# A linear-attention and two-mixture kernel: first mixture by 512 tokens in a written order, decays scanned from a chunk's head, memory taken from no shared pool, last four tiles routed inside the first expert

## The chip, the cores and the metric

The kernel runs on one NeuronCore of a Trainium2 chip. The metric is device time in microseconds of one execution; before the change the runs took 990.52, 990.67 and 990.67 us, median 990.67. Five engines work side by side, each through its own queue in order: TensorE (PE, whose weight loads are listed as PEld), VectorE (DVE), ScalarE (ACT), GpSimd (POOL) and SyncE (SP), which issues most DMAs.

## The reference

Three parts follow one another. All inputs are float32.

```
# 1. gated linear attention, batch 4, heads 8, 768 steps, head size 48
state = alpha[t][:, None] * state + outer(k[t], v[t])
y[t] = q[t] @ state                       # gives x: 3072 tokens x 384
# 2. first mixture: three projections to 768, their maximum, one back
h = max(x @ w1, x @ w2, x @ w3)           # 384 -> 768
x = h @ w_out                             # 768 -> 384
# 3. second mixture: 8 experts, the two largest noisy logits of each token
logits = x @ w_gate + log1p(exp(x @ w_noise)) * noise
out[token] += gate * (relu(x @ w1[e]) @ w2[e])     # 384 -> 1024 -> 384
```

## The kernel before

**Attention.** The sequence is cut into 24 units (j), two for each block of 256 tokens. `prep_a(j)` makes the decays with two scans on DVE: one backwards over the decays gives R (from each step to the end of its chunk of 64), a reciprocal of the chunk's product gives the start value of a second, forward one, D. R times the keys (POOL) and D times the queries (DVE, in `prep_x`) make a chunk's work a matmul. `r0`, the product over a chunk, times a decay of the input fills `AE` on POOL, the factors of the chunk-to-chunk scan. `att_t` transposes the keys on PE, `att_s` forms scores of 64 x 64 and masks them on DVE, `att_g` the contribution of each chunk to the state; there DVE scans the state over the chunks (L316), multiplies the result with `AE` (L319), and ACT copies it beside the values. `att_y` gives the output of a unit and splits it into a high and a low part, of reduced float32 (`FR`); for the odd unit six small DMAs (L348) put heads in their place.

**First mixture.** The weights come as float64 words. `wconv(i)`, i from 0 to 11, takes a piece through `dissect`: an absolute value on ACT, a maximum with TINY, a shift and two combinations on DVE (L164 to L167), a cast on ACT to the high part and a subtraction on POOL for the low part. `ffn(u, f)` multiplies block u (256 tokens) with one of six column groups f of three matrices: 3 x 9 matmuls of 256 columns (three contraction parts, each as high x high, high x low, low x high), each matrix into its own PSUM area; ACT copies the first, DVE takes two maxima, ACT casts, POOL subtracts. `proj(u, t)` projects 128 tokens back in 18 matmuls of 400 columns, the last 16 of which are the gate and noise logits.

**Routing.** Tiles of 128 tokens are routed six at a time, in four batches: softplus and noise (`route_a`, `route_b`), ranks within the experts by matmuls with triangular and all-one matrices (`route_c`, `route_r`), and a table of token numbers by one-hot matmuls (`route_h`, `route_m`). Tokens of rank below 384 come from a first table, finished after 18 tiles; the rest after the last batch.

**Second mixture.** Each expert is worked in two halves (n = 2e, 2e + 1) of 384 and 448 slots. `gather` fetches rows by indirect DMA, `turn` transposes them, `esplit` splits the weights, `up` and `down` multiply, and an indirect DMA adds the rows to the output. From n = 1 on a loop mixes the next half's gathers and transposes with this half's matmuls.

**What sets the order.** The program's text gives a sequence of calls for the start (L543 and after), then a loop over u, then a sequence from the last projections to the first expert. A planner of the tile framework puts each engine's instructions into a fixed order when the program is built, by priority (the text's order) and by when its own timing model finds them ready, so the order on an engine is near the text's but not the same. Semaphores do the rest at run time.

**Memory.** Pools are stacks of tiles. `at` holds what attention needs, and the raw pieces and scratch of `dissect` as well; it is closed in the last part of the loop, and `pr`, the experts' pool, takes its place. `pw` holds the first mixture's weights, `p2` the experts' weights after it.

Of the kernel before, what the change touches and what calls it, by code (L numbers as in the profile page):

```python
# [33 lines left out]
LATE = 2304  # L34

TINY = float(np.array([896 << 20], np.uint32).view(np.float32)[0])


@with_exitstack
def gla_moe_kernel(ctx: ExitStack, tc: tile.TileContext, qka, pad, vn, ws, wo, wgn, noise, e1, e2, out):  # L40
# [9 lines left out]
    pw = pw_cm.__enter__()  # L50
    at_cm = tc.tile_pool(name="at", bufs=1, side="right")
# [25 lines left out]
    Z = at.tile([128, 512], F32, name="Z")  # L77
    AE = [at.tile([128, 2, 48, 5], F32, name=f"ae{i}") for i in range(2)]
# [3 lines left out]
    H = ph.tile([128, 2, 6, 2, 256], FR, tag="h", name="H")  # L82
# [13 lines left out]
    def wload(i):  # L96
        if i in (2, 3, 4, 7, 8):
            wraw[i] = RAW[:, (i - 2) % 5]
        else:
            wraw[i] = at.tile([128, 1536], U32, tag="wraw", name="wraw", bufs=2)  # L100
        src = ws[i] if i < 9 else wo[i - 9]
        nc.sync.dma_start(wraw[i], src.bitcast(U32))

    for i in range(2):
        load(i)
        for g in range(2):
            nc.sync.dma_start(QKA[i][64 * g + 48:64 * g + 64], pad)
    for i in range(5):
        wload(i)
    nc.vector.memset(Z, 0.0)  # L110
# [9 lines left out]
    for i in range(2):  # L120
        nc.vector.memset(AE[i], 0.0)
# [35 lines left out]
    def dissect(raw, hi, lo):  # L157
        low, high = raw[:, :, 0], raw[:, :, 1]
        a = at.tile([128, 768], U32, tag="ca", name="ca", bufs=2)
        b = at.tile([128, 768], F32, tag="cb", name="cb", bufs=2)  # L160


        nc.scalar.activation(b, high.bitcast(F32), AF.Abs)
        nc.vector.tensor_scalar(b, b, TINY, None, op0=OP.max)  # L164
        nc.vector.tensor_scalar(a, b.bitcast(U32), 5, 2, op0=OP.logical_shift_left, op1=OP.logical_shift_right)
        nc.vector.scalar_tensor_tensor(a, high, 0xC0000000, a, op0=OP.bitwise_and, op1=OP.bitwise_or)
        nc.vector.scalar_tensor_tensor(a, low, 29, a, op0=OP.logical_shift_right, op1=OP.bitwise_or)  # L167
        f = a.bitcast(F32).rearrange("p (a d) -> p a d", a=2)
# [7 lines left out]
    def wconv(i):  # L176
# [20 lines left out]
    def gates_t(f):  # L197
# [24 lines left out]
    X1, X2, KH, KT, XT, ST, DD = {}, {}, {}, {}, {}, {}, {}  # L222

    parts = {}

    def used(j):
        parts[j] = parts.get(j, 0) + 1
        if parts[j] == 3 and j + 2 < 24:
            load(j + 2)

    def prep_a(j):
# [4 lines left out]

        R = KH[j] = at.tile([128, 512], F32, tag="kh", name="kh", bufs=2)
# [9 lines left out]
        nc.gpsimd.tensor_mul(AE[i][:, :, :, 1:5],  # L247
                             a0.rearrange("p (a b) -> p a b", a=2)[:, :, None, :].to_broadcast([128, 2, 48, 4]),
                             r0[:, :, None, :].to_broadcast([128, 2, 48, 4]))
        used(j)  # L250

    def prep_x(j):
# [18 lines left out]
    def prep_v(j):
# [25 lines left out]
    def att_g(j):  # L297
        i = j % 2

        ps = pa.tile([128, 2, 48, 5], F32, tag="a", name="psG")  # L300
# [9 lines left out]
        if (j // 2) % 3 == 0:  # L310
            nc.vector.memset(ps[:, :, :, 0], 0.0)
        else:
            nc.vector.tensor_copy(ps[:, :, :, 0], ST[j - 2][:, :, :, 4])
        st = at.tile([128, 2, 48, 5], F32, tag=f"S{i}", name="st")
        ST[j] = st
        nc.vector.tensor_tensor_scan(st.rearrange("q p e c -> q (p e c)"), AE[i].rearrange("q p e c -> q (p e c)"),  # L316
                                     ps.rearrange("q p e c -> q (p e c)"), 0.0, op0=OP.mult, op1=OP.add)

        nc.vector.tensor_mul(st[:, :, :, 0:4], st[:, :, :, 0:4], AE[i][:, :, :, 1:5])  # L319
        P = st[:, :, :, 0:4].rearrange("q p e c -> q p c e")  # L320
        nc.scalar.copy(LA[i][64:128, :, :, 0:48], P[64:128])  # L321
        nc.scalar.copy(LB[i][0:64, :, :, 0:48], P[0:64])

    def att_y(j):
        i, u = j % 2, j // 2
        ps = pa.tile([128, 2, 256], F32, tag="a", name="psY")
        for p in range(2):
            for c in range(4):
                s = slice(64 * c, 64 * c + 64)
                sx = slice(256 * p + 64 * c, 256 * p + 64 * c + 64)  # L330
                nc.tensor.matmul(ps[0:64, p, s], LA[i][:, p, c], X1[j][:, sx], start=True, stop=True)  # L331
                nc.tensor.matmul(ps[64:128, p, s], LB[i][:, p, c], X2[j][:, sx], start=True, stop=True)  # L332
        if i == 0:
            XT[u] = pw.tile([128, 3, 2, 256], FR, tag="xt", name="xt", bufs=2)
            x = XT[u]
            nc.scalar.copy(x[:, 0:2, 0, :], ps)
            nc.vector.tensor_sub(x[:, 0:2, 1, :], ps, x[:, 0:2, 0, :].bitcast(F32))
        else:
            x = XT[u]
# [3 lines left out]
            nc.scalar.copy(x[:, 2, 0, :], ps[:, 0])  # L343
            nc.vector.tensor_sub(x[:, 2, 1, :], ps[:, 0], x[:, 2, 0, :].bitcast(F32))

            for o in (0, 64):
                for k in range(3):
                    nc.sync.dma_start(x[o + 48:o + 64, k].bitcast(F32),  # L348
# [6 lines left out]
    def ffn(u, f):  # L355
        x = XT[u]
        p12 = pm.tile([128, 2, 256], F32, tag="p12", name="p12")
        p3 = pm.tile([128, 2, 256], F32, tag="p3", name="p3")
        for w, ps in ((0, p12[:, 0]), (1, p12[:, 1]), (2, p3[:, 0])):
# [5 lines left out]
        m = pw.tile([128, 256], F32, tag="m", name="m", bufs=2)  # L365
        nc.scalar.copy(m, p12[:, 0])  # L366
        nc.vector.tensor_max(m, p12[:, 1], m)  # L367
        nc.vector.tensor_max(m, p3[:, 0], m)  # L368
        hi = H[:, u % 2, f, 0]
        nc.scalar.copy(hi, m)  # L370
        nc.gpsimd.tensor_sub(H[:, u % 2, f, 1], m, hi.bitcast(F32))  # L371

    def proj(u, t):
        ps = pl.tile([128, 400], F32, tag="l2", name="psl2")
        n = 0
        for f in range(6):
            for a, b in THREE:
                nc.tensor.matmul(ps, H[:, u % 2, f, a, 128 * t:128 * t + 128], WOT[0][:, b, f],  # L378
                                 start=n == 0, stop=n == 17)
                n += 1  # L380
        i = 2 * u + t
# [27 lines left out]
    def route_b(b):  # L409
        t, l = RT[b]  # L410
        nl = NL[b]

        u = small([128, 6, NE], "u")
        d = small([128, 6, NE], "d")
# [5 lines left out]
        nc.vector.tensor_mul(l, l, nz[:, 6 * b:6 * b + 6, :])  # L420
        nc.vector.tensor_add(l, l, nl[:, :, 0:8])
        mx = small([128, 6, NE], "mx")
        ix = small([128, 6, NE], "ix", U32)
        for j in range(6):
            nc.vector.max(mx[:, j], l[:, j])
            nc.vector.max_index(ix[:, j], mx[:, j], l[:, j])
        xf = small([128, 6, 2], "xf")
        nc.vector.tensor_copy(xf, ix[:, :, 0:2])
        oh = small([128, 6, 2, NE], "oh")
        nc.vector.tensor_tensor(oh, iota[:, None, 0:NE].to_broadcast([128, 12, NE]).rearrange("p (j k) e -> p j k e", k=2),  # L430
                                xf[:, :, :, None].to_broadcast([128, 6, 2, NE]), op=OP.is_equal)
# [73 lines left out]
    def route_m(b, q):  # L505
# [7 lines left out]
        if q < 2:  # L513
            return
# [482 lines left out]
```

## Time and profile before

| what | value |
|---|---|
| median of the runs | 990.67 us |
| profiled execution | 989.96 us, its span 988.3 us |
| PE busy | 913.0 us, 92% of the span |
| DVE, ACT, POOL busy | 514.6, 389.5, 329.3 us |
| DMA | 88.22 MB, mean 89 GB/s |
| 72 feed-forward groups (L363) | 1944 matmuls, 254.7 us |
| experts, up (L792) and down (L806) | 1152 and 1344 matmuls, 242.5 and 243.3 us |

Busy times of engines overlap and do not add up to the span. A busy PE is one with a matmul in its pipeline; two matmuls start closer than each lasts, so a row's mean duration is not its cost: the distance of two starts is. Idle time of an engine costs nothing unless the last chain of work waits there.

### The profile page before, as it was taken

To read this page: it belongs to the slowest core of one execution; us is meant where nothing else is said; L and a number is where in the kernel's file an instruction comes from. 1 tells how busy PE (TensorE), PEld (TensorE's weight loads), DVE (VectorE), ACT (ScalarE), POOL (GpSimd) and SP (SyncE) were. 2 spreads that over 40 slices of the span, in tenths; PEclk is the share of its full clock that TensorE was granted. 3 is DMA by queue.
4 is the path that set the end of the run, shared out by engine and by line. 5 is a ranking of instruction groups with operands and counts; after the bars stand their busy time and mean duration, and the time that the engine had idled before them with its cause. 6 is when DMAs were issued, how large, how long until landed. Compare 5 with 4: busy or idle time off the path is not lost.

```text
span 988.3 us, 17871 instructions
## 1 busy us (share of the span) xinstructions
PE 913.0 (92%) x7186; PEld 866.7 (88%) x7187; DVE 514.6 (52%) x1040; ACT 389.5 (39%) x801; POOL 329.3 (33%) x362
## 2 busy tenths in 40 slices
PE   2358999999999999999898999999999999999994
PEld 2347999999999999999897999999999999999993
DVE  7999847786668865772573333322333323333110
ACT  3645454455445534632542333332333332333220
POOL 5477524322322332112108333333333233221112
PEclk9979899999999999999999999999999999999998
DMA  9642223134234232104325444334434434422112
GB/s 266 171 137 70 60 55 87 46 106 121 57 82 122 75 81 64 31 13 137 139 87 123 113 105 101 78 79 115 110 98 108 94 60 109 113 57 25 21 25 29
DMA packets 36693, 88.22 MB, mean 89 GB/s; under 512 B 8640, under 2 KB 25024, under 8 KB 36608
## 3 DMA queue, kind: packets, MB, share of 16 engines
q1 hardware_dynamic: 25600, 66.39, 23.7%
q0 software_dynamic: 11008, 20.67, 12.0%
q8 instruction: 57, 0.93, 0.4%
q14 instruction: 28, 0.23, 0.1%
HBM read 64.52 MB, written 20.16 MB: 86 GB/s over the span
## 4 chain that ended last, share of the span: by engine, by line
PE 74%; issue 4%; DMA 3%; DVE 2%; POOL 0%; ACT 0%; POOLq 0%; ACTq 0%; DVEq 0%
PE psd L806 21%; PE psu L792 21%; PE p L363 18%; PE psl L378 5%; DMA out_dram<-y,idx 2%; PE psx L773 2%; PE psS L290 1%; PE psG L306 1%; PE psY L331 1%; PE psT L282 1%; DMA xt<-sg 1%; PE psY L332 1%; DVE kh L239 0%; DVE x L259 0%; DMA xg<-x2d,idx 0%
## 5 line engine op out<-in xcount | busy, mean ns | idle before, releaser
L363 PE MATMUL p<-xt,W 128*128 128x256 f32 x1944 | 254.7, 289 | 9.9 <-DVE m L367 7.3
L363 PEld LDWEIGHTS p<-xt,W 128*128 128x128 f32 x1944 | 241.9, 195 | 15.0 <-DVE m L367 8.1
L792 PE MATMUL psu<-xe,ew 128*128 128x448 f32 (+1 forms) x1152 | 242.5, 358 | 4.3 <-ACT xe L775 4.3
L806 PE MATMUL psd<-ew,he 128*128 128x384 f32 (+1 forms) x1344 | 243.3, 335 | 0.0
L806 PEld LDWEIGHTS psd<-ew,he 128*128 128x128 f32 (+1 forms) x1344 | 227.0, 180 | 8.1 <-ACT y L809 0.2
L792 PEld LDWEIGHTS psu<-xe,ew 128*128 128x128 f32 x1152 | 208.2, 190 | 13.9 <-ACT xe L775 4.7
L796 DVE SCALAR_TENSOR_TENSOR he<-psu,he 128x448 fp32r<-128x448 f32 (+1 forms) x128 | 75.5, 590 | 265.0 <-ACT he L795 265.0
L811 POOL DMA_INDIRECT out_dram<-y,idx x56 | 88.1, 1573 | 187.8 <-ACT y L809 176.2
L371 POOL TENSOR_TENSOR H<-m,H 128x256 fp32r<-128x256 f32 x72 | 60.1, 835 | 191.2 <-ACT H L370 187.1
L809 ACT ACTIVATE y<-psd,GS 128x384 f32<-128x384 f32 (+1 forms) x56 | 32.4, 580 | 206.1 <-PE psd L806 195.2
L795 ACT ACTIVATE he<-psu 128x448 fp32r<-128x448 f32 (+1 forms) x128 | 66.3, 518 | 112.3 <-PE psu L792 112.3
L378 PE MATMUL psl<-WO,H 128*128 128x400 f32 x432 | 84.7, 349 | 0.0
L378 PEld LDWEIGHTS psl<-WO,H 128*128 128x128 f32 x432 | 76.7, 188 | 2.1 <-issue 1.3
L739 DVE TENSOR_TENSOR ew<-raw,ew 128x768 fp32r<-128x768 f32 x64 | 57.2, 954 | 33.6 <-ACT ew L738 32.9
L758 POOL DMA_INDIRECT xg<-x2d,idx x56 | 58.5, 1045 | 43.2 <-PE psx L773 21.2
L367 DVE TENSOR_TENSOR m<-p,m 128x256 f32<-128x256 f32 x72 | 29.9, 417 | 60.4 <-ACT m L366 59.9
L370 ACT CAST H<-m 128x256 fp32r<-128x256 f32 x72 | 29.2, 406 | 68.0 <-DVE m L368 66.2
L777 POOL COPY GS<-xg 128x1 f32<-128x1 f32 (+1 forms) x56 | 10.8, 272 | 124.2 <-DMA xg<-x2d,idx 124.2
L366 ACT COPY m<-p 128x256 f32<-128x256 f32 x72 | 26.4, 369 | 61.6 <-PE p L363 58.4
L738 ACT CAST ew<-raw 128x768 fp32r<-128x768 f32 x64 | 48.6, 831 | 3.2 <-DMA raw<-in_e_dram 3.2
L331 PE MATMUL psY<-x,la 128*64 128x64 f32 x384 | 31.5, 237 | 15.6 <-ACT la L321 14.9
L331 PEld LDWEIGHTS psY<-x,la 128*64 128x64 f32 x384 | 27.1, 148 | 19.7 <-ACT la L321 15.7
(151 smaller groups left out, 1080.0 us busy)
## 6 DMA issues: line engine op xcount, KB each, us to landing
raw<-in_e_dram SPq DMA_DIRECT2D x32, 768.0 KB, 5.6
qka<-in_qka_dram SPq DMA_DIRECT2D x48, 289.7 KB, 4.7
out_dram<-z SPq DMA_DIRECT2D x5, 960.0 KB, 4.5
vn<-in_vn_dram SPq DMA_DIRECT2D x24, 192.0 KB, 2.6
x2d<-x2t SPq DMA_DIRECT2D x24, 192.0 KB, 1.9
RAW<-in_ws_dram SPq DMA_DIRECT2D x5, 768.0 KB, 10.8
wraw<-in_ws_dram SPq DMA_DIRECT2D x4, 768.0 KB, 8.6
xt<-sg SPq DMA_DIRECT2D x72, 32.0 KB, 3.5
```

The costliest lines, as they stand in the source:

```text
L331: nc.tensor.matmul(ps[0:64, p, s], LA[i][:, p, c], X1[j][:, sx], start=True, stop=True)
L363: nc.tensor.matmul(ps, W[:, f, w, a, k], x[:, k, b], start=n == 0, stop=n == 8)
L371: nc.gpsimd.tensor_sub(H[:, u % 2, f, 1], m, hi.bitcast(F32))
L378: nc.tensor.matmul(ps, H[:, u % 2, f, a, 128 * t:128 * t + 128], WOT[0][:, b, f], start=n == 0, stop=n == 17)
L738: nc.scalar.copy(hi, r)
L739: nc.vector.tensor_sub(EW[e, m][:, 1, s], r, hi.bitcast(F32))
L758: nc.gpsimd.indirect_dma_start(out=XG[n, i][0:w], out_offset=None, in_=x2d if h else x2d[0:128 + LATE], in_offset=bass.IndirectOffsetOnAxi ...
L792: nc.tensor.matmul(ps, w[:, a, f, k], XE[n][:, k, b], start=i == 0, stop=i == 8)
L795: nc.scalar.activation(hi, ps, AF.Relu)
L796: nc.vector.scalar_tensor_tensor(HE[n][:, f, 1], ps, 0.0, hi.bitcast(F32), op0=OP.max, op1=OP.subtract)
L806: nc.tensor.matmul(ps, HE[n][:, f, a, o:o + m], w[:, b, f], start=j == 0, stop=j == 23)
L811: nc.gpsimd.indirect_dma_start(out=out, out_offset=bass.IndirectOffsetOnAxis(ap=IDX[h][0:m, 1, c:c + 1], axis=0), in_=y, in_offset=None, c ...
```

## The change

The start-up: the first two units come from a new input, `qk2`, already padded to 128 partitions, in three DMAs each (decays, keys, queries); the pad's DMAs and the memory clearing of `AE` on DVE go. Later loads hang on `prep_x` (queries, keys, decays) and `prep_v` (values) separately. The decays: the forward scan D now runs first and starts from the chunk's first decay; the reciprocal of its last value starts the backward scan. `AE` (now one tile) holds the chunk products alone, filled by ACT; the state's scan adds, then multiplies, so that the product after it goes. The maximum of `dissect` moves to POOL, and scratch and raw pieces get memory of their own. The feed-forward runs over 512 tokens (d from 0 to 5), in one matmul each, except d = 0 and f = 0, 1 of d = 1, which run as two halves. H lies in eight places. Routing has five batches (6, 6, 6, 2 and 4 tiles). The calls stand as words in three lists: a, x, v, t, s, g, y are the attention's functions, w `wconv`, f `ffn`, p `proj`, i and j the gates, z `zero_rows`, r the next routing step; in the last list L, G, E, T, U, D are `eload`, `gather`, `esplit`, `turn`, `up`, `down` and A, B, C, R, H, M the routing of the last four tiles. The last list is run under a manual schedule for PE, DVE and ACT: their instructions keep the text's order.

```diff
+BATCH = (0, 6, 12, 18, 20, 24)
+HANDOVER = """
+    L0.0.0 L0.0.1 L0.1.0 G0.0 G0.1 G0.2 E0.0.0 E0.0.1 p5.0 E0.0.2 E0.0.3 p5.1 T0.0 T0.1 T0.2 E0.1.0 E0.1.1
+    p5.2 E0.1.2 E0.1.3 p5.3 A4 B4 U0.0 U0.1 U0.2 C4 R4 U0.3 H4.0 U0.4 H4.1 U0.5 M4.0 U0.6 M4.1
+    G1.0 G1.1 G1.2 G1.3 G2.0 G2.1 G2.2 U0.7 D0.0 D0.1 T1.0 T1.1 D0.2 T1.2 T1.3
+"""
+ORDER = """
+    a0 x0 t0 a1 s0 v0 g0 x1 s1 a2 t1 y0 v1 x2 g1 a3 y1 w0 v2 w1 w2 t2 s2 x3 g2 v3 w3 w4 t3 s3 y2 g3 a4
+    x4 v4 y3 f0.0.0 w5 f0.1.0 w6 f0.2.0 w7 f0.3.0 t4 s4 w8 f0.4.0 a5 g4 x5 v5 f0.5.0 w9 t5 s5 f0.0.1 a6
...
+    v14 f2.3 z1 r t14 s14 f2.4 r a15 y13 g14 x15 v15 f2.5 r t15 s15 a16 y14 g15 x16 v16 y15 t16 s16
+    f3.0 z2 a17 g16 x17 v17 f3.1 t17 s17 p2.0 a18 y16 g17 x18 v18 p2.1 t18 s18 p2.2 a19 y17 g18 x19 v19
...
+ORDER2 = """
+    f5.0 f5.1 p4.0 p4.1 r p4.2 r r p4.3 r r f5.2 r r f5.3 r r f5.4 r r f5.5 r r
 def load(j):
-        for g in range(2):
-            nc.sync.dma_start(QKA[i][64 * g:64 * g + 48], qka[j, g])
-        nc.sync.dma_start(VN[i].rearrange("p a b c e -> p (a b c e)"), vn[j])
+            for a, b in ((1024, 1545), (512, 1024), (0, 512)):
+                nc.sync.dma_start(QKA[i][:, a:b], qk2[j, :, a:b])
 def dissect(raw, hi, lo):
-        a = at.tile([128, 768], U32, tag="ca", name="ca", bufs=2)
-        b = at.tile([128, 768], F32, tag="cb", name="cb", bufs=2)
+        b = cv.tile([128, 768], F32, tag="cb", name="cb", bufs=2)
+        a = b.bitcast(U32)
-        nc.vector.tensor_scalar(b, b, TINY, None, op0=OP.max)
+        nc.gpsimd.tensor_scalar(b, b, TINY, None, op0=OP.max)
 def prep_a(j):
-        nc.vector.memset(Z[:, 0:512:64], 1.0)
-        nc.vector.tensor_tensor_scan(R[:, ::-1], al[:, 512:0:-1], Z, 0.0, op0=OP.mult, op1=OP.add)
-        nc.vector.reciprocal(Z[:, 0:512:64], R[:, 0:512:64])
-        nc.vector.tensor_tensor_scan(D, al[:, 0:512], Z, 0.0, op0=OP.mult, op1=OP.add)
-        nc.gpsimd.tensor_copy(r0.rearrange("p a b -> p (a b)"), R[:, 0:512:64])
+        nc.vector.tensor_copy(Z[0][:, 0:512:64], a0)
+        nc.vector.tensor_tensor_scan(D, al[:, 0:512], Z[0], 0.0, op0=OP.mult, op1=OP.add)
+        nc.vector.reciprocal(Z[1][:, 63:512:64], D[:, 63:512:64])
+        nc.vector.tensor_tensor_scan(R[:, ::-1], al[:, 512:0:-1], Z[1][:, ::-1], 0.0, op0=OP.mult, op1=OP.add)
         nc.gpsimd.tensor_mul(R, t[:, 512:1024], R)
-        nc.gpsimd.tensor_mul(AE[i][:, :, :, 1:5],
...
+        nc.vector.tensor_copy(EN[j].rearrange("p a b -> p (a b)"), D[:, 63:512:64])
 def att_g(j):
+        nc.scalar.copy(AE[:, :, :, 1:5], EN[j][:, :, None, :].to_broadcast([128, 2, 48, 4]))
+        nc.vector.memset(ps[:, :, :, 0], 0.0)
+        if not first:
+            before = ST[j - 2][:, :, :, 4]
+            nc.scalar.copy(LA[i][64:128, :, 0, 0:48], before[64:128])
+            nc.scalar.copy(LB[i][0:64, :, 0, 0:48], before[0:64])
+            nc.vector.tensor_add(ps[:, :, :, 1], ps[:, :, :, 1], before)
-        nc.vector.tensor_mul(st[:, :, :, 0:4], st[:, :, :, 0:4], AE[i][:, :, :, 1:5])
-    def ffn(u, f):
+    def ffn(d, f, half=None):
+        s = slice(0, 512) if half is None else slice(256 * half, 256 * half + 256)
+        for w in range(3):
+            ps = pm.tile([128, 512], F32, tag="p", name="p", bufs=4)[:, s]
...
+    run(ORDER)
+    at_cm.__exit__(None, None, None)
+    pr = ctx.enter_context(tc.tile_pool(name="pr", bufs=1, side="right", reuse_waits="tile"))
+    run(ORDER2)
...
+    with tc.manual_schedule(engines={mybir.EngineType.PE, mybir.EngineType.DVE, mybir.EngineType.Activation}):
+        run(HANDOVER)
```

## Rows read from the trace of the kernel before

**Rows 1.** The page: span, and PE's busy time.
```profile
span 988.3 us, 17871 instructions
...
PE 913.0 (92%) x7186; PEld 866.7 (88%) x7187; DVE 514.6 (52%) x1040; ACT 389.5 (39%) x801; POOL 329.3 (33%) x362
```

**Rows 2.** Busy time by stretch: start and end, length, engines' busy us (count), clock, DMA.
```profile
0.00:110.00 110.00, 59.63 (x610) 54.49 (x611) 102.66 (x134) 49.97 (x92) 65.64 (x66) 0.89 0.57 153
...
160.00:460.00 300.00, 296.96 (x3151) 282.25 (x3150) 209.24 (x517) 141.06 (x323) 86.53 (x110) 1.00 0.32 82
...
480.00:530.00 50.00, 42.94 (x244) 39.74 (x242) 31.17 (x109) 22.92 (x44) 9.60 (x10) 0.95 0.44 139
```

**Rows 3.** Timeline of the first 12.5 us, DVE's first scan.
```profile
8.57 1.23 DVE L239 TENSOR_TENSOR_SCAN kh<-qka,Z 128x512 f32<-128x512 f32 x1 [5.22 <-DMA qka<-in_pad_dram]
```

**Rows 4.** DMA view of 0 to 30 us, rate in 40 slices of 0.75 us.
```profile
GB/s 0 0 115 338 181 187 123 199 239 181 190 157 187 129 160 296 156 238 401 451 401 410 418 418 426 418 401 426 410 377 370 198 165 194 125 224 224 157 189 144
```

**Rows 5.** DVE's groups, 0 to 110 us: count, busy us, mean ns, idle before.
```profile
L242 DVE TENSOR_TENSOR_SCAN D<-qka,Z 128x512 f32<-128x512 f32 x7 | 13.3, 1902 | 0.1
...
L164 DVE TENSOR_SCALAR cb<-cb 128x768 f32<-128x768 f32 x11 | 8.0, 723 | 0.0
...
L319 DVE TENSOR_TENSOR st<-st,ae 128x384 f32<-128x384 f32 x5 | 4.5, 892 | 0.0
...
L313 DVE COPY psG<-st 128x96 f32<-128x96 f32 x3 | 1.0, 317 | 0.0
...
L238 DVE MEMSET Z<- 128x8 f32 x8 | 0.5, 65 | 0.0
```

**Rows 6.** POOL's groups, 0 to 110 us.
```profile
L170 POOL TENSOR_TENSOR W<-ca,W 128x768 fp32r<-128x768 f32 x9 | 19.4, 2166 | 16.7 <-ACT W L169 16.7
...
L247 POOL TENSOR_TENSOR ae<-qka,r 128x384 f32<-128x384 f32 x6 | 9.5, 1591 | 0.8 <-DVE st L319 0.5
...
L244 POOL COPY r<-kh 128x8 f32<-128x8 f32 x7 | 5.2, 742 | 17.9 <-DVE kh L239 17.9
...
L123 POOL MEMSET la<- 64x512 f32 x2 | 1.0, 520 | 0.1
```

**Rows 7.** Timeline of DVE and of POOL near 40 us.
```profile
39.79 2.09 DVE L164 TENSOR_SCALAR cb<-cb 128x768 f32<-128x768 f32 x1
...
38.75 2.71 POOL L170 TENSOR_TENSOR W<-ca,W 128x768 fp32r<-128x768 f32 x1
```

**Rows 8.** Chain that ended last: start, length, what, count of instructions.
```profile
460.12 19.45 PE p L363 x162
...
580.33 4.18 PE psd L806 x24
584.51 1.85 PE psu L792 x9
```

**Rows 9.** Timeline of PE at the last of these, with its columns.
```profile
584.35 1.81 PE L792 MATMUL psu<-xe,ew 128*128 128x448 f32 x8
```

**Rows 10.** Timeline of PE in the handover, idle before in brackets.
```profile
479.39 3.43 PE L378 MATMUL psl<-WO,H 128*128 128x400 f32 x18
...
494.21 8.15 PE L792 MATMUL psu<-xe,ew 128*128 128x384 f32 x36 [3.89 <-ACT xe L775]
...
524.26 0.52 PE L773 MATMUL psx<-ident,xg 128*128 128x128 f32 x3 [1.31 <-DMA xg<-x2d,idx]
...
528.05 1.54 PE L792 MATMUL psu<-xe,ew 128*128 128x448 f32 x4 [0.41 <-ACT xe L775]
```

**Rows 11.** Timeline of the last batch's routing: first on ACT, one-hot sums on DVE.
```profile
494.41 0.26 ACT L404 ACTIVATE r_t<-nl 128x48 f32<-128x48 f32 x1
...
504.52 0.20 DVE L433 TENSOR_TENSOR r_ob<-r_oh 128x48 bf16<-128x48 f32 x1
```

**Rows 12.** Chain that ended last, near 350 us.
```profile
347.10 0.38 ACT m L366
...
347.99 5.97 DMA xt<-sg
```

More of the change, by code (lines that the diff above doesn't have):

```diff
@@ L105, in gla_moe_kernel @@
         load(i)
-        for g in range(2):
-            nc.sync.dma_start(QKA[i][64 * g + 48:64 * g + 64], pad)
+        load_v(i)
     for i in range(5):
         wload(i)
-    nc.vector.memset(Z, 0.0)
+    for z in Z:
+        nc.vector.memset(z, 0.0)
     nc.gpsimd.memset(ident, 1.0)
@@ L119, in gla_moe_kernel @@
     nc.vector.memset(VBD, 0.0)
-    for i in range(2):
-        nc.vector.memset(AE[i], 0.0)
+    nc.gpsimd.memset(AE, 0.0)
     for i in range(2):
@@ L333, in att_y, with att_y_lo @@
+        if i == 0 and u % 2 == 0:
+            XT[d] = XW2[d % 2]
+    def att_y_lo(j):
+        i, u = j % 2, j // 2
+        d, s = u // 2, slice(256 * (u % 2), 256 * (u % 2) + 256)
+        ps = YP.pop(j)
         if i == 0:
[L334 to L337, printed above, removed]
+            x = XT[d][:, 0:2, :, s]
+            nc.scalar.copy(x[:, :, 0], ps)
+            nc.vector.tensor_sub(x[:, :, 1], ps, x[:, :, 0].bitcast(F32))
@@ L364, in ffn, with proj @@
                     n += 1
[L365 to L369, printed above, removed]
+            if w == 0:
+                nc.scalar.copy(m, ps)
+            else:
+                nc.vector.tensor_max(m, ps, m)
+        hi, lo = (place(d, f)[:, a, s] for a in range(2))
         nc.scalar.copy(hi, m)
-        nc.gpsimd.tensor_sub(H[:, u % 2, f, 1], m, hi.bitcast(F32))
-    def proj(u, t):
+        nc.gpsimd.tensor_sub(lo, m, hi.bitcast(F32))
+    def proj(d, t):
         ps = pl.tile([128, 400], F32, tag="l2", name="psl2")
@@ L410, in route_b @@
         t, l = RT[b]
[L411 to L414 removed]
+        n = BATCH[b + 1] - BATCH[b]
+        nl = NL[b][:, 0:n]
+        u = row("u", b, NE)
+        d = row("d", b, NE)
         nc.vector.tensor_scalar(u, t, 1.0, None, op0=OP.add)
@@ L465, in route_r @@
         xf, oh, rk, ct = RT[b]
-        rb = small([128, 6, NE], "rb")
+        n = BATCH[b + 1] - BATCH[b]
+        rb = row("u", b, NE)
         if b == 0:
@@ L511, in route_m @@
             A, C = held.pop(0)
-            nc.tensor.matmul(ps[:, 0:n], A, C[:, 0:n], start=q == 0 and i == 0, stop=q == 2 and i == 3)
-        if q < 2:
+            nc.tensor.matmul(ps[:, 0:n], A, C[:, 0:n], start=q == 0 and i == 0, stop=q == last and i == 3)
+        if q < last:
             return
@@ new lines, in gla_moe_kernel, with run @@
+    steps = []
+    CALL = {"a": prep_a, "x": prep_x, "v": prep_v, "t": att_t, "s": att_s, "g": att_g, "y": att_y, "w": wconv,
+            "f": ffn, "p": proj, "i": gates_t, "j": gates_m, "z": zero_rows, "c": late_consts}
+    def run(order):
+        for word in order.split():
+            if word == "r":
+                while steps and next(steps[0], steps) is steps:
+                    steps.pop(0)
+                continue
+            args = [int(n) for n in word[1:].split(".") if n]
+            CALL[word[0]](*args)
+            if word[0] == "p" and 4 * args[0] + args[1] + 1 in BATCH:
+                steps.append(routing(BATCH.index(4 * args[0] + args[1] + 1) - 1))
```

488 lines of the change are left out of this document (157 added, 331 removed).

## The prediction

> **What bounds the kernel now.** I read the page first. Its span is 988.3 us and TensorE (PE) is busy for 913.0 of it [rows 1]. So PE is the bound, and a change can only save time in two ways: fewer or faster matmul columns, or fewer PE holes. The second view, busy time by stretch, says where the holes are [rows 2]. From 160 to 460 us PE is busy for 296.96 of 300 us at a granted clock of 1.00 (2.4 GHz; the 0.89 of the first 110 us mixes that level with 1.2 GHz): nothing there is to be had but speed of the matmuls themselves. In the first 110 us PE is busy for 59.63 and VectorE (DVE) for 102.66: the start-up belongs to DVE, which never rests. Between 480 and 530 us, where the mixture hands over to the experts, PE is busy for 42.94 of 50. After that come the experts, whose steady loop the diff leaves alone (only the name of four PSUM banks changes), and I give them nothing.
>
> **Step 1, the first transfer.** The first scan on DVE starts at 8.57 us and has waited 5.22 us for the pad's DMA, the last of five [rows 3]. The change sends the decays (521 of 1545 columns, all 128 partitions, 267 KB) ahead as one DMA; the first scan now needs only these. By the DMA view 86 KB had moved by 2.25 us and 340 KB by 3.0 (115 and 338 GB/s in slices of 0.75 us) [rows 4]. With about 1 us until the queue's receipt wakes DVE I take 4.3 us for the scan's start, which is 4.3 us earlier; the ends are 0 (the pieces share the rings as before) and 5.2 (the whole wait goes). The k and q pieces, 262 KB each at some 190 GB/s, land 1.4 us after one another, within the 2.7 us that the two scans and the reciprocal take.
>
> **Step 2, DVE's work in the start-up.** Of the rows of DVE up to 110 us [rows 5] two disappear: the maximum with TINY (L164, 11 in this stretch, 8.0 us), which moves to GpSimd (POOL), and the product of the state with the decays (L319, 5, 4.5 us), which the scan with the operations in the order add, multiply now yields by itself. New on DVE are a copy of 8 columns per unit in place of a memset of 65 ns, another of 8 columns, and, where a state is carried in, a memset beside an addition of 96 columns that takes the place of a 317 ns copy. A new 8-column operation lies between 65 ns (that memset) and 317 ns (the copy of 96); I take 100 ns, near the memset of its own size, 7 x 100 = 0.7 us, and 0.6 for the carried states: 1.3 us. Net 12.5 - 1.3 = 11.2 us off an engine that has no hole, while PE waits for it; as long as PE starves, that is time. Two guards. First, POOL: its rows lose the copy of r (L244, 7, 5.2 us) and the product for ae (L247, 6, 9.5 us), 14.7 us together, and gain 11 maxima of 768 columns [rows 6]. One of these is bounded by 0.78 us (a memset of 512 columns takes 520 ns, by columns) and 2.17 us (the subtraction of two inputs, L170); 1.3 us, because it reads one input and not two, gives 14 us. So POOL's load stays as it is. That matters since POOL slows DVE: the same maximum took 2.09 us on DVE while POOL's L170 ran for 2.71 us [rows 7], against a mean of 723 ns [rows 5], and the D scan's mean of 1902 ns is of the same origin. With equal POOL load I leave DVE's other rows as they are. Second, ScalarE (ACT) takes over the filling of ae (a copy of 384 columns per unit) and small copies for the carried state; it is busy 49.97 of 110 us [rows 2], so I cost them at nothing; if DVE's order put them ahead of the state's copies, each would delay one unit by under a microsecond. Ends for this step: 0 (POOL holds DVE up for what it takes over) and 20 (POOL's removal also frees DVE's other rows).
>
> **Step 3, 512 tokens in one matmul.** Feed-forward d = 0 runs in halves, and so do f = 0 and 1 of d = 1; the other 28 (4 of d = 1, 24 of d = 2 to 5) are full width: 28 x 27 = 756 matmuls of 512 columns in place of 1512 of 256. The chain of work has 162 of 256 columns in 19.45 us, 120.1 ns each, 24 of 384 in 4.18 us, 174.2 ns, and nine of 448 in 1.85 us, 205.6 ns [rows 8, 9]. No row has 512. From 256 to 384 a column costs 0.42 ns, which gives 174.2 + 54 = 228 ns; in proportion to 448 it is 235 ns, in proportion to 256 it is 240. I take 231, between the two nearest rows: each pair saves 2 x 120.1 - 231 = 9.2 ns, 756 x 9.2 = 7.0 us, with ends 0 and 9.2. All of it is on PE, in the stretch where PE has no hole, so it counts in full. Evictions on ACT and DVE are fewer and longer; DVE is at 209 of 300 us there [rows 2], which covers them. The projections, the attention's matmuls and the gates keep their counts.
> The Trainium skill (TensorE: Matmul & The Clock Gate, Back-to-back issue gap) gives the isolated warm gap as N / 2.4 + 2.5 ns. By it a pair costs 2 x 109.2 and one of 512 costs 215.8, an estimate from that page, so a pair saves 2.6 ns and the step 2.0 us. The trace does not agree at 256 columns, 120.1 ns [rows 8].
>
> **Step 4, the handover.** From the first projection after the last feed-forward to the first matmul of the second half-expert PE takes 528.05 - 479.39 = 48.7 us, with holes of 3.89 (for xe, whose cast stands on ACT behind weights that had not landed), 1.31 us (for the first of the gathers, which start after the routing's end), three of under 0.7 for the others, and 0.41 [rows 10]: some 7 us. The written order sets the transposes before the last two projections, and the gathers under two down-projections, 4.2 us each [rows 8]; that ends both kinds. It also fixes PE, DVE and ACT in one order, with new waits: the rank matmuls of the last 4 tiles stand behind three up-groups (3 x 9 x 174 ns = 4.7 us), while their input needs two table loads and some 16 DVE operations. In the trace of before that took from 494.41 to 504.72 us [rows 11], 10.3 us for 6 tiles; for 4 I take 4/6 of it, 6.9, a hole of 2.2 us, and 2.5 more for the two places where the table's matmuls wait for DVE's one-hot rows. Behind the waiting rank matmul on PE stand all up-groups, and behind DVE's wait the evictions that free the four banks. 7 - 4.7 = 2 us gained, rounded. Ends: 7 (no new hole) and -10 (the chain is not covered at all).
>
> **Sum.** 988.3 - 4.3 - 11.2 - 7.0 - 2.0 = 963.8 us of span. The profiled execution took 989.96 us, 1.7 beside its span, and the median of the runs is 990.67, 0.7 above it: 963.8 + 1.7 + 0.7 = 966 us.
>
> **Rivals.** (a) POOL eats the start-up. If a maximum on POOL costs what L170 does, 11 x 2.17 = 23.9 us replace 14.7, and DVE is held up by them; for it speaks the 2.09 us of [rows 7]. Step 2 is then worth nothing: 977 us. Against it: one input only, and r and ae are gone from the same unit's path.
> (b) More than forecast. If a one-input POOL instruction leaves DVE alone, the loss of r and ae (14.7 of POOL's 65.64 us [rows 2, 6]) frees DVE: the D scans have a mean of 1.90 us where the first scan, with POOL idle, took 1.23 [rows 3, 5], 7 x 0.67 = 4.7 us. With all holes of step 4 gone another 5, and wide matmuls at 228 ns another 2: 954 us.
> (c) The spacing goes with the columns alone, so that one of 512 takes what two of 256 do, 240 ns: step 3 is worth nothing, 973 us. The fixed part in the rows of 256 and 384 (0.469 and 0.454 ns a column) speaks against it. The Trainium skill's gap rule, weighed in step 3, is close to it: 971 us, an estimate.
> (d) Slower: each block of 512 tokens waits for its last x. A full-width group can't start before four units are through, and the last of these ends in six small DMAs; once in the trace the chain went from 347.10 to 353.96 us through an eviction and such a DMA [rows 12], 6.9 us. If PE has nothing to put under it at the five block starts (d = 1 to 5), that is 34 us against 24.5 gained: 1000 us. It decides from the fourth uncovered block on (27 us). For it: in the written order the last unit of d = 3 stands right ahead of that block's first group. Against it: four projections of the block before (3.43 us each [rows 10]) wait to be run there, and in the other blocks at least one full group lies between.
> That the written order is not followed is no rival by itself: outside the handover the planner places instructions by its own timing, and there PE is full anyway.
>
> **How the numbers follow.** Forecast (956 to 975 us) 0.40, (a) 0.22, (b) 0.20, (c) 0.08, (d) 0.10. Range 946 to 986: it holds (a), (b) and (c) and leaves out (d), with some room for ends beyond the cases. A measurement of this kernel can tell 0.2%, 2 us. Faster 0.87 (all but (d), less what of (a) ends at no gain), same 0.03, slower 0.10.
>
> **What would show it.** Step 1: the first scan at 4 to 5 us. Step 2: no product behind the state's scan on DVE, DVE's rows up to 95 us some 11 us lighter, and PE full from about 95 us instead of 110; wrong, if POOL's maximum shows 2 us or DVE's D scan grows beyond 1.9 us. Step 3: 27 matmuls of a full-width group in 6.2 us. Step 4: the time from the first projection after the last feed-forward to the second half-expert, less one projection, 47 us. The forecast is wrong if PE shows holes over 3 us at a block's start, waiting for x, or over 5 us in the handover, waiting for DVE.

## The result, and the profile after

The changed kernel takes 982.4 us (median of four runs, 981.70 to 983.48) against 990.67: ratio 0.9905, interval 0.9886 to 0.9925. The forecast was 966, a gain of 24.7 us; the gain is 8.3. The sign is right, the size a third. The profiled execution took 981.72 us, with a span of 980.0.

Busy time by stretch comes first, with the columns of [rows 2]: the kernel after, then the row of before for 110 to 160 us, which the forecast had not looked at.

```profile
0.00:110.00 110.00, 67.06 (x702) 59.73 (x703) 99.19 (x137) 59.97 (x117) 79.86 (x64) 0.84 0.54 153
110.00:160.00 50.00, 44.06 (x518) 40.86 (x518) 39.35 (x64) 30.58 (x68) 24.11 (x21) 0.97 0.32 73
160.00:460.00 300.00, 297.24 (x2413) 250.60 (x2412) 186.71 (x476) 139.96 (x300) 54.13 (x46) 1.00 0.30 77
480.00:530.00 50.00, 44.67 (x251) 42.63 (x250) 28.15 (x94) 19.72 (x39) 18.23 (x26) 0.97 0.51 140
```

```profile
110.00:160.00 50.00, 48.89 (x530) 47.06 (x531) 29.72 (x52) 25.76 (x58) 19.98 (x19) 1.00 0.20 53
```

POOL went from 65.64 to 79.86 us in the first 110, DVE only from 102.66 to 99.19. And in 110 to 160 us, where PE had been full before, it now has 5.9 us of holes instead of 1.1. The granted clocks of the first 110 us (0.89 before, 0.84 after) can't be compared: from 0 to 40 us the kernel before reads 1.00, yet a pair of its score matmuls (64 x 64) takes 107 ns at 14.4 us and 58 ns at 316 us.

How far one kernel is ahead of the one before is read by a **lead**: each matmul is given its usual distance to the next at full clock (120 ns for 256 columns, 240 for 512, counted as the two that it replaces, 182 for 400, 109 for 128, some 30 for one of 64 columns, and so on), these are added up from the start, and the lead at a time is how much later the kernel before had as much behind it. After is ahead by 8.1 us at 20 us, 6.5 at 100, and **4.9 us behind at 160**; then it comes to +5.5 at 460 and +8.9 at 540, and little moves after that (8.5 at 950). The lead at 160 us moves by about 1 us with the prices of the small matmuls, since the new order has run more of them by then; from 460 us on it does not. The start-up, forecast to end 15.5 us ahead, ended behind; the stretch of the wide matmuls (160 to 460 us) gave 10.4 and that of the handover (460 to 540 us) 3.4.

DVE's start, by the timeline (compare [rows 3]); POOL's groups and DVE's groups up to 110 us (compare [rows 5, 6]); and what PE waited for up to 160 us (us in total, times, longest):

```profile
3.81 0.17 DVE L275 COPY Z<-qka 128x8 f32<-128x8 f32 x1 [0.94 <-DMA qka<-in_qk_dram]
4.01 1.22 DVE L277 TENSOR_TENSOR_SCAN D<-qka,Z 128x512 f32<-128x512 f32 x1
```

```profile
L205 POOL TENSOR_SCALAR cb<-cb 128x768 f32<-128x768 f32 x11 | 32.4, 2949 | 7.2 <-ACT cb L204 7.2
L211 POOL TENSOR_TENSOR W<-cb,W 128x768 fp32r<-128x768 f32 x9 | 18.2, 2025 | 3.9 <-ACT W L210 3.9
```

```profile
L206 DVE TENSOR_SCALAR cb<-cb 128x768 uint32<-128x768 uint32 x10 | 12.5, 1252 | 4.6 <-POOL cb L205 4.5
L277 DVE TENSOR_TENSOR_SCAN D<-qka,Z 128x512 f32<-128x512 f32 x8 | 12.4, 1546 | 0.1
...
L275 DVE COPY Z<-qka 128x8 f32<-128x8 f32 x9 | 4.1, 459 | 2.5 <-DMA qka<-in_qka_dram 1.6 <-DMA qka<-in_qk_dram 0.9
...
L283 DVE COPY en<-D 128x8 f32<-128x8 f32 x8 | 2.8, 355 | 0.0
```

```profile
PE psT L323 <- POOL kh L281: 22.5, 3, 8.6
PE psY L383 <- ACT la L366: 12.0, 5, 4.7
```

The maximum (L205) takes 2.95 us on POOL, more than the subtraction of two inputs beside it. DVE's shift (L206) waits for it, and POOL's product for the keys (L281) is queued behind it: PE's transposes wait 22.5 us for that product. The first of these three waits, 8.6 us, is the start itself: POOL's first maximum comes at 14.7 us. So the maximum can have a part in 13.9 us of it, not in all.

### The profile page after: what moved, and what is told of

Same layout as the page of the kernel before. It is cut to its first block, busy times and chain, and to the rows that moved or that the text cites. A ratio compares the mean times of both kernels' runs of the same rounds, so it can differ in the third digit from the quotient of the medians.

```text
span 980.0 us, 16245 instructions
## 1 busy us (share of the span) xinstructions
PE 908.2 (93%) x6431; PEld 825.8 (84%) x6432; DVE 499.2 (51%) x1014; ACT 400.6 (41%) x806; POOL 317.6 (32%) x299
## 4 chain that ended last, share of the span: by engine, by line
PE 76%; DVE 7%; DMA 6%; issue 2%; ACT 1%; POOL 1%; SPq 0%; POOLq 0%; DVEq 0%; ACTq 0%
PE psd L742 22%; PE psu L728 21%; PE p L432 18%; PE psl L447 6%; DMA qka<-in_qka_dram 3%; DMA out_dram<-y,idx 2%; PE psY L383 2%; PE psx L709 2%; PE psS L331 1%; DVE x L291 1%; PE psG L349 1%; PE psT L323 1%; DVE st L363 1%; DMA raw<-in_e_dram 1%; DVE x L334 1%
## 5 line engine op out<-in xcount | busy, mean ns | idle before, releaser
L432 PE MATMUL p<-xt,W 128*128 128x512 f32 (+1 forms) x1188 | 247.2, 362 | 6.4 <-DVE m L437 3.2
L432 PEld LDWEIGHTS p<-xt,W 128*128 128x128 f32 x1188 | 197.6, 194 | 39.1 <-DVE m L437 3.5
L440 POOL TENSOR_TENSOR H<-m,H 128x512 fp32r<-128x512 f32 (+1 forms) x34 | 43.0, 1264 | 117.1 <-ACT H L439 117.0
L437 DVE TENSOR_TENSOR m<-p,m 128x512 f32<-128x512 f32 (+1 forms) x88 | 51.7, 588 | 48.5 <-PE p L432 40.5
L447 PE MATMUL psl<-WO,H 128*128 128x400 f32 x336 | 68.3, 348 | 0.0
L281 POOL TENSOR_TENSOR kh<-qka,kh 128x512 f32<-128x512 f32 x24 | 33.6, 1399 | 106.5 <-issue 31.8
L447 PEld LDWEIGHTS psl<-WO,H 128*128 128x128 f32 x336 | 60.1, 188 | 1.6 <-issue 0.5
L383 PE MATMUL psY<-x,la 128*64 128x64 f32 x384 | 33.6, 239 | 12.9 <-ACT la L366 12.0
L383 PEld LDWEIGHTS psY<-x,la 128*64 128x64 f32 x384 | 27.9, 148 | 18.1 <-ACT la L366 13.2
L439 ACT CAST H<-m 128x512 fp32r<-128x512 f32 (+1 forms) x34 | 18.5, 545 | 55.2 <-DVE m L437 55.1
```

The source lines that it names most:

```text
L383: nc.tensor.matmul(ps[0:64, p, sc], LA[i][:, p, c], X1[j][:, sx], start=True, stop=True)
L432: nc.tensor.matmul(ps, W[:, f, w, a, k], x[:, k, b], start=n == 0, stop=n == 8)
L437: nc.vector.tensor_max(m, ps, m)
L447: nc.tensor.matmul(ps, place(d, f)[:, a, 128 * t:128 * t + 128], WOT[0][:, b, f], start=n == 0, stop=n == 17)
```

## The experiments

Times against the kernel before, run beside them on the same chip; lead at 160, 460 and 540 us, and PE's idle time up to 160 us (160 less its busy time), from one profiled execution each. The runs of one kernel spread by up to 10 us (lazy 989.78 to 1000.07, max_dve 975.75 to 983.02), and the profiled execution is not always near the median: it took 983.05 us in planned, 983.36 in warm, 991.33 in old_decays and 975.75 in max_dve. Two kernels count as different here where their intervals lie apart.

| kernel | us | ratio, interval | leads | idle |
|---|---|---|---|---|
| before | 990.5 to 991.7 | 1 | 0, 0, 0 | 51.5 |
| after | 982.40 | 0.9905, 0.9886 to 0.9925 | -4.9, 5.5, 8.9 | 48.9 |
| max_dve | 977.45 | 0.9881, 0.9860 to 0.9902 | 1.5, 11.5, 14.5 | 41.3 |
| no_max | 977.48 | 0.9850, 0.9829 to 0.9870 | 2.8, 13.6, 12.2 | 41.3 |
| before_pool | 998.18 | 1.0079, 1.0064 to 1.0093 | -4.5, -4.5, -8.1 | 54.5 |
| halves | 995.73 | 1.0046, 1.0031 to 1.0060 | -4.4, -3.9, -5.5 | 48.9 |
| lazy | 992.42 | 1.0020, 1.0003 to 1.0036 | -1.2, -6.1, -2.9 | 42.7 |
| copies_act | 977.07 | 0.9860, 0.9839 to 0.9882 | 4.3, 9.6, 12.8 | 42.4 |
| old_decays | 987.80 | 0.9982, 0.9962 to 1.0002 | -7.9, -3.5, -0.6 | 47.8 |
| planned | 979.31 | 0.9883, 0.9866 to 0.9899 | -9.2, 0.9, 6.8 | 49.5 |
| first_load | 983.48 | 0.9917, 0.9903 to 0.9931 | 7.5, 7.7, 7.8 | 44.1 |
| warm | 977.92 | 0.9854, 0.9839 to 0.9870 | see there | 37.6 |
| best | 973.76 | 0.9819, 0.9805 to 0.9833 | 0.1, 10.1, 14.6 | 43.0 |
| load_decays | 988.22 | 0.9971, 0.9949 to 0.9994 | 9.0, -0.3, 0.2 | 44.2 |
| old_order | 975.18 | 0.9841, 0.9824 to 0.9858 | -2.0, 8.0, 13.2 | 39.5 |

**max_dve, no_max, before_pool: who takes the maximum.** The edit of max_dve; no_max drops the line, and before_pool is the reverse in the kernel before.

```diff
-        nc.gpsimd.tensor_scalar(b, b, TINY, None, op0=OP.max)
+        nc.vector.tensor_scalar(b, b, TINY, None, op0=OP.max)
```

> The changed kernel with one edit: the maximum of the splitting helper goes back from POOL to DVE. Theory A (POOL's maximum, 2.95 us each, holds POOL's k products and with them TensorE's transposes in the first 110 us): PE's wait for POOL's kh (22.5 us in three waits) shrinks to under 8 us, the first mixture matmul comes 6 to 12 us earlier than 54.9, and the time falls to 970 to 976 us. Rival B (the written order and the other edits of the start-up set its length, whoever takes the maximum): first mixture matmul within 3 us of 54.9, time 980 to 984 us. Rival C (DVE is the tighter engine there, so the move to POOL helped after all): 985 to 995 us.

> The changed kernel with the maximum of the splitting helper left out altogether (a weight under the smallest normal number is then not lifted to it, a part of the computation that is left out). Neither POOL nor DVE has it. Theory A: the whole cost of the maximum goes, 966 to 974 us, a few us under the kernel that has it on DVE. Rival B (order and other edits): 979 to 983 us.

> The kernel before with one edit, the converse: its maximum goes from DVE to POOL. Theory A: POOL's maximum takes 2 to 6 us there as well, POOL goes from 66 to about 90 us busy in the first 110 us, the k products come late: 998 to 1008 us against 990.7. Rival B: no change or, since DVE was the tighter engine there, faster: 982 to 991 us.

The direction of theory A holds both ways: on POOL the maximum costs the changed kernel 5.0 us by the medians and the kernel before 7.6 (998.18 against 990.54, although DVE lost a row there). The intervals of after and max_dve overlap; the clear pair is planned and best, below, which differ in this line alone: 979.31 against 973.76, 5.5 us, with intervals apart. It is not all of it. 977.45 lies between the ranges of A and B, and so does the first mixture matmul, which comes at 50.0 us, 4.9 earlier. PE still waits 18.8 us for POOL's kh in max_dve, 8.5 of them at the start, and leaving the maximum out gives no more than taking it back to DVE (the intervals overlap). So the maximum is the smaller part of the 20.4 us (15.5 forecast, -4.9 found) that the start-up is missing. The waits of max_dve up to 160 us, then before_pool's row on POOL, 0 to 110 us:

```profile
PE psT L323 <- POOL kh L281: 18.8, 3, 8.5
```

```profile
L164 POOL TENSOR_SCALAR cb<-cb 128x768 f32<-128x768 f32 x11 | 28.1, 2554 | 4.5 <-ACT cb L163 4.5
```

**halves: the wide matmul alone.**

```diff
 def ffn(d, f, half=None):
+    if half is None:
+        ffn(d, f, 0)
+        ffn(d, f, 1)
+        return
```

> The changed kernel with every block of the first mixture run as two of 256 tokens (same order, same weights; 256 columns per matmul again). If the gain between 160 and 460 us is the wider matmul (756 pairs, 2 x 120 ns against 227 ns), the time grows by 9 to 12 us to 991 to 995 us. If that gain comes from the order and the other edits, it stays at 982 to 985 us.

13.3 us slower than after. The order and the start-up are the same (lead -4.4 at 160), and the lead stands still from 160 to 460 us, where after gains 10.4: that is the width. Not all of the 13.3 us is. By the leads halves is 9.4 us behind after at 460 and 14.4 at 540; the other 5.0 lie in the stretch of the handover, where PE waits 3.41 us for xe ahead of the second half-expert and in after 1.21.

**planned and best: the handover.** best has the maximum on DVE as well.

```diff
-with tc.manual_schedule(engines={mybir.EngineType.PE, mybir.EngineType.DVE, mybir.EngineType.Activation}):
-    run(HANDOVER)
+run(HANDOVER)
```

> The changed kernel with its last list of calls run without the manual schedule, so that the planner orders PE, DVE and ACT there as it does elsewhere. Forecast's step 4: the handover with the fixed order takes 47.2 us against 48.7 before, a gain of 1.5 us; without it the time is 982 to 986 us. If the fixed order holds engines behind one another (3.7 us at the rank matmuls): 977 to 981 us.

> The changed kernel with two edits: the maximum on DVE (5.0 us faster alone) and the last list of calls without the manual schedule (3.1 us faster alone). The two lie in different stages: if both are additive, 974 to 975 us, under both kernels. If one of the two was the spread between runs: 977 to 979 us.

The fixed order costs 3.1 us by the medians, with intervals that overlap; max_dve and best, which differ in it alone, are 3.7 us apart and so are their intervals.

Planned's profile shows one thing more. PE, DVE, ACT and POOL run the same instructions in the same order as in after up to 474 us, yet at 160 us this execution (983.05 us; the others took 978.72 to 979.53) is 9.2 us behind and not 4.9. Its row for 110 to 160 us has PE as busy as in after, yet with 464 matmuls in place of 518, at a granted clock of 0.86 and not 0.97:

```profile
110.00:160.00 50.00, 44.36 (x464) 40.82 (x463) 37.06 (x61) 27.54 (x62) 25.10 (x20) 0.86 0.30 69
```

So a stretch at the lower clock that comes in one execution and not in another costs some 4 us here, with nothing changed in the program before it.

PE's holes in the handover, timeline of after, compare [rows 10]:

```profile
470.25 1.26 PE L447 MATMUL psl<-WO,H 128*128 128x400 f32 x6
...
478.94 0.55 PE L709 MATMUL psx<-ident,xg 128*128 128x128 f32 x3 [0.96 <-DVE xe L712]
...
494.44 0.19 PE L519 MATMUL psr<-r_ob,tri 128*128 128x32 bf16 x1 [3.67 <-DVE r_ob L508]
...
501.57 0.24 PE L591 MATMUL pstab<-r_C,r_A 128*128 128x192 f16 x1 [0.20 <-DVE r_C L579]
...
520.86 1.08 PE L728 MATMUL psu<-xe,ew 128*128 128x448 f32 x4 [1.21 <-ACT xe L711]
```

and of planned:

```profile
474.83 1.26 PE L447 MATMUL psl<-WO,H 128*128 128x400 f32 x6
...
490.08 6.65 PE L728 MATMUL psu<-xe,ew 128*128 128x384 f32 x36 [0.58 <-ACT xe L711]
...
521.35 6.13 PE L728 MATMUL psu<-xe,ew 128*128 128x448 f32 x21 [0.41 <-ACT xe L711]
```

Planned, PE is through from the first of the last four projections to the second half-expert in 46.5 us; in the fixed order it takes 50.6 (520.86 - 470.25), and the 3.67 us at the rank matmul are gone. The gains add up: best, at 973.76, has both (982.40 - 5.0 - 3.1 = 974.3) and is the fastest kernel here.

**first_load: step 1 alone, in the kernel before.** The core of the edit; the pad's transfers go as well.

```diff
+if j < 2:
+    for a, b in ((1024, 1545), (512, 1024), (0, 512)):
+        nc.sync.dma_start(QKA[i][:, a:b], qk2[j, :, a:b])
```

> The kernel before with one part of the change alone: the first two units come from the padded input in three pieces each (decays first), and the pad's transfers go. The forecast's step 1: the first scan starts at about 4 instead of 8.6 us and all of it shifts the start-up, 986 to 987 us. Rival G (DVE at 103 of 110 us is filled up later anyway, the 4.5 us are lost in the waits of the units behind): 989 to 992 us.

8.2 us, as much as the whole change gives, and it is kept: the lead is 7.5 at 160 us and stays. The first scan starts here at 3.60 us, 5.0 earlier; how 5 became 8 stays open (the pad's transfers are gone too), but rival G is wrong.

```profile
3.60 1.23 DVE L241 TENSOR_TENSOR_SCAN kh<-qka,Z 128x512 f32<-128x512 f32 x1 [0.25 <-DMA qka<-in_qk_dram]
```

**old_decays, copies_act, load_decays: the decays.** The first puts `prep_a` and the state scan of before into after; the second sets L275 and L283 of max_dve on ACT; the third adds the new decays to first_load. The core of old_decays, and copies_act:

```diff
-nc.vector.tensor_tensor_scan(st..., ps..., AE..., 0.0, op0=OP.add, op1=OP.mult)
+nc.vector.tensor_tensor_scan(st..., AE[i]..., ps..., 0.0, op0=OP.mult, op1=OP.add)
+nc.vector.tensor_mul(st[:, :, :, 0:4], st[:, :, :, 0:4], AE[i][:, :, :, 1:5])
```

```diff
-nc.vector.tensor_copy(Z[0][:, 0:512:64], a0)
+nc.scalar.copy(Z[0][:, 0:512:64], a0)
```

> The changed kernel (maximum on POOL) with the decays as before: backward scan first, chunk products on POOL (a copy of 0.6 us and a product of 1.4 us a unit in the profile of before), and the product after the state scan on DVE (0.8 us a unit). If the new decays give what the forecast said, about 0.6 us of DVE and 2 us of POOL a unit, and POOL with the maximum is what holds the start-up, undoing them costs 6 to 12 us: 988 to 994 us. If they gave nothing (the new 8-column copies eat it): 981 to 985 us.

> The changed kernel with the maximum on DVE and the two 8-column copies of each unit (L275, L283) on ACT. Theory E (these copies, 0.36 to 0.55 us each beside POOL where 0.12 us is their shortest, take 10.6 us of DVE in 0 to 160 us, and DVE is the bound there): DVE's busy time in 0 to 110 us falls by 6 to 8 us and the time to 969 to 974 us. Rival F (ACT's copy comes late in its own queue and the decay scan waits for it): 978 to 985 us.

> The kernel before with two parts of the change: the first load (8.2 us faster alone, 983.5) and the new decays (forward scan first, chunk products on ACT, no product after the state scan). If the new decays are worth the 5 us that undoing them in the changed kernel cost: 977 to 980 us. If that worth came only from POOL being full there (91 us of its 110 with the maximum), and the two 8-column copies on DVE eat the rest: 982 to 985 us.

Undoing the decays costs 5.4 us, at the edge of what was expected. Taking the small copies off DVE brings nothing: DVE's busy time falls by 2.4 us only (105.31 to 102.93 up to 110 us), so both theories on them miss. In the order of before the new decays leave the start-up slightly further ahead (9.0 at 160), but nearly all of it is lost between 160 and 340 us (0.8), where PE, full there before, is busy for 292.01 us of the 300 up to 460: load_decays is 4.7 us slower than first_load. So the decays gain in the one order and lose in the other; no run shows why.

**lazy, old_order: the written order.** lazy holds units 4 to 7 back and runs d = 1 in halves, in max_dve; old_order gives best the calls of the kernel before up to the first projections. From the first feed-forward on, the old order, lazy and then old_order; the rest of the lists is left out:

```diff
- f0.0.0 w5 f0.1.0 w6 f0.2.0 w7 f0.3.0 t4 s4 w8 f0.4.0 a5 g4 x5 v5 f0.5.0 w9 t5 s5 f0.0.1 a6
+ f0.0.0 w5 f0.1.0 w6 f0.2.0 w7 f0.3.0 w8 f0.4.0 t4 s4 f0.5.0 a5 g4 x5 v5 f0.0.1 w9 f0.1.1
...
+ f0.0.0 s3 a4 f0.1.0 w6 x4 w7 t4 w8 f0.2.0 f0.3.0 f0.4.0 w9 y3 f0.5.0 f0.3.1 f0.4.1 v4 s4
```

> The changed kernel with the maximum on DVE and another written order up to the first whole block of 512 tokens after the second: the twelve feed-forward halves of d = 0 run as soon as their weights are there, units 4 to 7 come two to three halves later each, and all six groups of d = 1 run as halves (4 more groups, 4 x 27 pairs at 13 ns = 1.4 us dearer). Theory B (with the maximum back on DVE, 977.4 us, what is still missing of the start-up went because the written order brings two more units ahead by 110 us, 7 against 5 before, while DVE is the bound at 105 of 110 us): PE's lead at 160 us grows from 1.5 us to 7 to 12, and the time falls to 967 to 973 us. Rival D (DVE's total work to the end of the start-up is what counts, in whatever order): 976 to 980 us.

> The fastest so far (changed kernel, maximum on DVE, last list planned: 973.8 us) with the order of the kernel before from the start to the first projections: units 4 to 7 three to five feed-forward halves later, weights earlier, the rest of the list as it was. Its lead at 160 us was 0 to 1.5 us, that of the kernel before with the new first load 7.5 us. Theory B' (the written order of the start-up loses the difference): the lead at 160 us goes to 5 to 8 us, 966 to 970 us. Rival (the decays, buffers or the clock lose it, in whatever order): 972 to 977 us; if attention then comes late for the blocks of 512, more.

Both miss. lazy is 15 us slower than max_dve, most of it from my own list: in 220 to 240 us PE is busy for 11.52 of 20, behind late units of attention. Neither brings the lead at 160 us up, so the order is not shown to be the cause. What they show instead is in the stretches of old_order, then those of max_dve:

```profile
110.00:125.00 15.00, 12.35 (x157) 11.05 (x157) 12.59 (x20) 10.12 (x22) 10.17 (x8) 1.00 0.07 19
125.00:145.00 20.00, 18.35 (x146) 16.91 (x147) 7.59 (x13) 6.11 (x14) 3.32 (x4) 0.57 0.28 61
145.00:160.00 15.00, 15.00 (x115) 14.02 (x114) 6.97 (x12) 6.88 (x17) 1.32 (x1) 1.00 0.57 172
```

```profile
125.00:145.00 20.00, 18.00 (x215) 16.34 (x215) 16.92 (x26) 13.93 (x35) 12.11 (x10) 1.00 0.30 74
```

old_order has the least PE idle time up to 160 us of the kernels without added work (39.5) and was 8.9 us ahead at 120. From 125 to 145 PE is as busy as in max_dve, with 146 matmuls instead of 215, at a granted clock of 0.57, mostly its lower level of 1.2 GHz, after 15 us with PE busy for 12.35. At 140 it is 0.5 us behind. In the kernel before, PE is busy for 14.58 of 15 us from 110 to 125 and the clock then stays at 1.00. But holes alone don't bring the clock down: in after PE is busy for 15.79 of the 20 us from 125 to 145, and the clock reads 1.00 there and in the 15 us behind.

**warm: the clock.** In max_dve:

```diff
 ps = bank(j, "psT", True)
+if 2 <= j <= 4:
+    for _ in range(24):
+        nc.tensor.transpose(ps[:, 0:128], ident, ident)
```

> The changed kernel with the maximum on DVE, and 24 further 128 x 128 transposes of the identity (whose result is overwritten) ahead of those of units 2, 3 and 4, where TensorE waits 18.8 us for POOL's kh. Theory H (with the maximum on DVE PE's idle time in 0 to 160 us is 10.2 us less than before, but its lead is only 1.5 us, because the clock stands at its lower level, 1.2 GHz, in parts of 25 to 120 us and the same work takes longer): PE busy in the waits keeps the granted clock of 40 to 110 us over 0.9 instead of 0.8, and the time falls by 2 to 5 us to 972 to 975. Rival (the clock there costs nothing, since PE waits anyway): 977 us, or up to 5 us more where the added transposes outlast the waits.

No change in time, but the theory was not tested: the clock hardly rose. From 40 to 110 us, where 0.9 was expected, it is 0.83 in max_dve and in warm. From 30 to 80 us, max_dve, then warm:

```profile
30.00:80.00 50.00, 33.09 (x326) 29.43 (x324) 49.36 (x69) 25.61 (x52) 21.32 (x11) 0.72 0.44 114
```

```profile
30.00:80.00 50.00, 35.89 (x345) 32.01 (x345) 49.46 (x70) 25.45 (x52) 20.13 (x11) 0.76 0.47 124
```

Its lead of 7.2 at 160 us counts 7.9 us of added work; without it, -0.7.

## Why the prediction was wrong, step by step

**Step 1** was right at its place (first scan at 4.01 us, forecast 4.3) and too small as a price: alone it is worth 8.2 us.

**Step 2 is the step that failed, in two terms.** "1.3 us, because it reads one input and not two" was 2.95: POOL's 11 maxima took 32.4 us, not 14, so "POOL's load stays as it is" became 14.2 us more. The bounds, 0.78 and 2.17, did not even hold the mean; at 2.17 the rival (a), whose mechanism came true, was priced at 977. And "100 ns" for an 8-column copy was 459 and 355: 6.9 us for 17 of them, not 0.7 for seven; its nearest row in size was a memset, which is another operation. Of 11.2 us that DVE was to lose, its busy time up to 110 us lost 3.5 (with eight decay scans in that stretch, though, where the kernel before had seven), and DVE gained 4.5 us of waiting for POOL. max_dve, before_pool and the pair of planned and best show the maximum's part: 5.0, 7.6 and 5.5 us. For the copies no price in time is shown: copies_act takes them off DVE and gains nothing.

**What also failed is the sentence that DVE's relief, "as long as PE starves, that is time".** In max_dve PE's idle time up to 160 us is 10.2 us less than before, and the lead there is 1.5. The forecast looked at the start-up as if it ended at 110 us. In 110 to 160 us the kernel before was full (1.1 us of holes) at the full clock; after has holes of 5.9 us, most of them waiting for units of attention, and a clock of 0.97. There its lead falls from some 5 us to -4.9. The rows account for 6.3 of these 10 us: 4.8 us more of holes, and 0.03 of 50 us of clock, 1.5 us. The rest is not assigned. old_order loses 9 us from 120 to 140 us, most of it at the low clock. first_load, which keeps the order and the decays of before, keeps its lead through it.

**Step 3** was right in kind and low in size. The chain of after:

```profile
260.20 6.34 PE p L432 x27
...
318.50 5.25 PE p L432 x23
```

Second row: 228 ns each; the first holds the last one's way out as well. The median distance of two starts is 227 ns, a hair under the lowest of the three extrapolations (228): 2 x 120.1 - 227 = 13.2 ns, x 756 = 10.0 us, forecast 7.0. The lead from 160 to 460 us agrees (10.4); halves, 13.3 us slower, holds a longer handover besides. Rival (c) is out. Where the gap rule of the Trainium skill (TensorE: Matmul & The Clock Gate, Back-to-back issue gap) would have given 2.0 us, an estimate, the measurement decides.

**Step 4** came out as forecast: 50.6 less one projection of 3.4 is 47.2 us (forecast 47), with 3.67 us at the rank matmuls (forecast 2.2) and under 0.5 at the table's (forecast 2.5). The mistake was the comparison: without the fixed order the same calls take 4.1 us less.

**Rival (d)** did not come: from 160 to 460 us PE is busy for 297.24 of 300, and its longest wait there is 0.9 us, so no block of 512 waited for its last x.

**The parts don't add up.** First load 8.2, the width's 10.0, less the maximum's 5.0 and the fixed order's 3.1 make 10.1, with the decays' 5.4 it is 15.5 (18.8 with the 13.3 of halves); 8.3 was measured. Each part is a difference of medians, good to some 2 us. Much of the gap lies before 160 us: first_load has a lead of 7.5 there, best 0.1. So of the 20.4 us that the start-up is missing, the maximum explains some 5 and the rest is open. The two profiles of one program up to 474 us, after and planned, put some 4 us on a stretch at the lower clock, but no run held the clock up; taking back the order of the calls, or taking the two small copies off DVE, did not bring the lead back.

## What to carry to other kernels

Before work is moved to POOL, look for a row of that operation on POOL; a row of another operation is no bound. Price a start-up up to the first stretch in which the bound engine is full in the kernel before, and check that stretch after the change: holes that appear there cost themselves, and a stretch at the lower clock, where it comes, some 4 to 9 us more in these runs. Run each part of a bundled change by itself: here one part alone gives as much as all together, and two cost 8 us.

## What the hardware showed

- A maximum with a constant over 768 columns, one input, took 2.12 us on POOL at its shortest and up to 5.97 us beside a busy DVE, more than a subtraction of two inputs (2.03 us mean). On DVE it is 0.72 [rows 5].
- A DVE copy of 8 columns takes 0.11 us at its shortest, but is held by POOL: in max_dve, by the timelines of POOL and of DVE, the copy ends (40.00) when POOL's subtraction does (39.98).

```profile
36.47 3.51 POOL L211 TENSOR_TENSOR W<-cb,W 128x768 fp32r<-128x768 f32 x1 [2.29 <-ACT W L210]
```

```profile
38.35 1.65 DVE L283 COPY en<-D 128x8 f32<-128x8 f32 x1
```

The Trainium skill (SBUF — State Buffer, Who interferes with whom) has it that DVE in its two-port modes and GpSimd take a shared pair of ports in turns, the first for its whole instruction, the other blocked. These rows agree, to 20 ns; that the copy ran in such a mode, no run shows.

- A matmul of 512 columns costs 227 ns where two of 256 cost 240.
